# Column 128 moved beside the sine columns, with the padding of the weights gone and three steps moved

## The chip, the cores and the metric

The kernel runs on one core of a Trainium2 chip. The metric is the time of one execution in microseconds as the device measures it. The engines are named as in the profile: PE is the matrix engine (PEld its weight loads), DVE the vector engine, ACT the scalar engine, POOL the GpSimd engine, SP the queue that starts most transfers.

## The reference

For each of eight batches x is 3136 by 256 in float32. The reference takes the real part of the Fourier transform along both axes, and puts the result through a mixer: a low-rank step along the 3136 rows (rank 32, matrices U and V) and a two-layer perceptron along the 256 columns (hidden width 1024, ReLU), each with its residual.

```python
X = np.fft.fft(x, axis=1)
X = np.fft.fft(X, axis=2)
x = X.real.astype(np.float32)
...
xt = x.transpose(0, 2, 1)
h = xt @ U @ V
u = x + h.transpose(0, 2, 1)
ch = np.maximum(u @ w_ch1, 0.0) @ w_ch2
return (u + ch).astype(np.float32)
```

## The kernel before

The real part of a two-dimensional transform of real data is even under reflection, so sums and differences of mirrored elements ("folds") cut the work down. Along the 256 columns the folds leave 127 differences (sine columns) and 129 sums (cosine columns 0 to 128). Along the 3136 rows further folds split the data into quarters: `EOF_` and `EOR_` hold the column folds of the forward and reversed rows, `EOS` the next fold, `GE` and `GO` its even and odd halves, and `GC` (two tiles) the last fold of `GE`. PE then multiplies `GC` and `GO`, as weights of 128 columns, with tables of sines and cosines (`TABE`, `TABO`, `TABS`), on whose ends the transformed U is appended, so that the same products give the low-rank step's first factor.

The columns of the folded tiles are laid out as 0 to 127 sine (column 0 zero), 128 to 256 cosine 0 to 128, column 257 zero, and up to width `GW` = 384 zeros. The weights are taken in three groups: columns 0 to 127 (`typ` 0), 128 to 255 (`typ` 1), and 256 to 383, of which only column 256 holds data. The third group is used in `seq(b, 1, 0, .)`, `even_rows(b, 0, .)` and `u_alone(0, 0, .)`, directly behind products of `typ` 0, into the same PSUM tile.

The work is staged as follows. A front, written out in order (`tc.manual_schedule()`), makes the tables from `krow` by phases on DVE and sines on ACT, transforms U (`flip_u`, `fold_u`, `transform_u`), folds batch 0 and transforms it. On PE, `fill(n)` issues n matmuls whose result nobody reads, between the steps of the front. Behind it the output is made in 25 chunks of up to 512 folded rows. For each chunk c, `direct` and `mirrors` make the hidden layer (with `front` making the chunk's input u and `odd_part` the difference `uo` that `mirrors` reads), `second_product` the second layer, and `store` writes the result. Between these steps `turn(c, slot)` issues the steps that `put` filed under slot 6c + slot: the folds of later batches at the places in `FOLDS`, and the transform of a batch at the slots that `transform(b)` returns. Matmuls and the folds keep their program order; other operations are ordered by the framework's scheduler.

```python
iota(krow[:, 2 * NT:4 * NT], [[-2, 2 * NT]], 783)
...
todo = products(b, par, typ, P * typ, pn == 1, ne)
if typ == 0 and b == 0:
    todo = todo + products(b, par, 1, 256, (pn == 1) == (par == 1), ne)
elif typ == 0 and pn == 1:
    todo = todo + [(QW, w, rhs) for w, rhs in u_odd(b, 1, 256)]
```

All matmuls behind the front go through the helper at line 463, so in the profile they have one line and are told apart by tiles: pt and ptu are the transform's, pst the step along the columns, ph the low-rank step, p the two layers.

Of the kernel before, what the change touches and what calls it, by code (L numbers as in the profile page):

```python
# [27 lines left out]
GW = 384  # L28
# [3 lines left out]
def kernel(  # L32
# [94 lines left out]
    iota(krow[:, 2 * NT:4 * NT], [[-2, 2 * NT]], 783)  # L127
# [15 lines left out]
    iota(jv[:], [[1, KP]], 0, 1)  # L143
# [19 lines left out]
    for t in (EOF_, EOR_):  # L163
        nc.vector.memset(t.rearrange("p a i d -> p (a i) d")[:, :, 0:258:257], 0.0)
# [3 lines left out]

    def zeros(eng, s):
        eng.memset(GO[s].rearrange("p a i d -> p (a i) d")[:, :, 258:GW].bitcast(I32), 0)  # L170
        for c in range(2):
            eng.memset(GC[s][c][:, :, 258:GW].bitcast(I32), 0)

# [36 lines left out]
    def phase_even(i):  # L210

        y, col = phe[:, i // 2], ncol[:KP, i:i + 1]
        for part, src in ((slice(0, NT), strip(krow[:KP], NT // 2, [[NT, 2], [1, NT // 2]])),
                          (slice(NT, 2 * NT), krow[:KP, 3 * NT:4 * NT])):
            dst = y[:, part].bitcast(FP32)
            if part.start == 0:
                dst = dst.rearrange("p (a j) -> p a j", a=2)
            nc.vector.tensor_scalar(dst, src, col, float(2 ** (23 - 15)), op0=AL.mult, op1=AL.add)
        nc.vector.tensor_single_scalar(y, y, 2 ** 15 - 1, op=AL.bitwise_and)
# [24 lines left out]
    def flip_u():  # L244
        nc.vector.tensor_single_scalar(J[:], jv[:], 97.0, op=AL.is_equal)
        nc.vector.scalar_tensor_tensor(J[:], jv[:], 196.0, J[:], op0=AL.is_equal, op1=AL.add)
        pf = psum.tile([KP, 4, NI, R], FP32, tag="p1", name="pf", bufs=BUFS["p1"])
        nc.tensor.matmul(pf.rearrange("p q i r -> p (q i r)"), J[:],  # L248
                         UA.rearrange("p q i r -> p (q i r)"), start=True, stop=True)
        return pf  # L250

    def fold_u(UF):
        for t in range(2):
            op = AL.add if t else AL.subtract
            nc.vector.tensor_tensor(uy[:, t, 0].rearrange("p a (i r) -> p a i r", r=R),
                                    UF[:, 0:4:2], UR[:, 3::-2, ::-1], op=op)
            nc.vector.tensor_tensor(uy[:, t, 1].rearrange("p a (i r) -> p a i r", r=R),
                                    UR[:, 0:4:2, ::-1], UF[:, 3::-2], op=op)
# [58 lines left out]
    def transform_u(t, fill=None):  # L317
# [46 lines left out]
        def evict():  # L364
# [4 lines left out]
                                 pu[:KP, 6:8, :].rearrange("p c r -> p (c r)"), AF.Copy, scale=hv[:KP])  # L369
            nc.scalar.copy(TABO[t].rearrange("p n i w -> p (n i) w")[:PQ, :, 2 * NT:WO], pu[:PQ, 8:12, :])  # L370
# [3 lines left out]
        return even_k, odd_k, evict  # L374
# [41 lines left out]
    def along_d(qs, src, dst, part):  # L416
# [18 lines left out]
    def half(b, par, cols):  # L435
# [3 lines left out]
        if par and b:  # L439
            ins = nc.vector.tensor_copy(dst[:, :, :, 0], dst[:, ::-1, :, 256])  # L440
# [70 lines left out]
    def products(b, par, t, col, odd, ne):  # L511

        mm = []
        if par == 0:
            for c in range(2):
                g = GC[b % 2][0 if (c == 0) == (t == 1) else 1]
                lo, hi, at = ((0, TE - NT + ne, 0), (T2 - ne, WE, TE - NT))[c]
                for i in ((0, 2) if odd else (1, 3)):
                    mm.append((at, g[:kp(i), i, col:col + P], TABE[t][:kp(i), i, lo:hi]))
        else:  # L520
            for i in ((0, 2) if odd else (1, 3)):
# [4 lines left out]
                for nm in range(2):  # L526
                    mm.append((at, GO[b % 2][:kp(i), nm, i, col:col + P],
# [3 lines left out]
    def u_odd(b, t, col):  # L531

        todo = []
        for i in range(NI):
            tab, lo = (TABS[t], off_u(t, i)) if i % 2 else (TABO[t], 2 * NT)
            todo += [(GO[b % 2][:kp(i), nm, i, col:col + P], tab[:kp(i), nm, i // 2, lo:lo + NE])
# [3 lines left out]
    def add_up(pt, todo):  # L540
        for n, (at, w, rhs) in enumerate(todo):
            mm(pt[:, at:at + rhs.shape[-1]], w, rhs, start=(n == 0), stop=(n == len(todo) - 1),
               skip_group_check=True)

    def seq(b, par, typ, pn, tag="dft", part=True):
# [5 lines left out]
        todo = products(b, par, typ, P * typ, pn == 1, ne)  # L551
# [53 lines left out]
    def even_rows(b, typ, pn, tag="dft"):  # L605
# [6 lines left out]
        todo = products(b, 0, typ, P * typ, pn == 1, ne)  # L612
        if typ == 0:
            todo = todo + products(b, 0, 1, 256, pn == 0, ne)
        for n, (at, w, rhs) in enumerate(todo):
            mm(pt[:, at:at + rhs.shape[-1]], w, rhs, start=(pn == 0 and n == 0),
# [27 lines left out]
    def u_alone(b, typ, kept, odd=True, even=True):  # L644
# [4 lines left out]
        for t, col in ((1, P),) if typ else ((0, 0), (1, 256)):  # L649
            if odd:  # L650
                todo += u_odd(b, t, col)
            for c in range(2) if even else ():
                g = GC[b % 2][0 if (c == 0) == (t == 1) else 1]
                lo = TE - NT + NE * c
                todo += [(g[:kp(i), i, col:col + P], TABE[t][:kp(i), i, lo:lo + NE]) for i in range(NI)]
        at = typ * R
        for n, (w, rhs) in enumerate(todo):
            mm(kept["pt"][:, at:at + R], w, rhs, start=(odd and n == 0), stop=(even and n == len(todo) - 1),
# [5 lines left out]
    def even_first(b, typ):  # L664
# [3 lines left out]
        todo = products(b, 0, typ, P * typ, False, 0) + products(b, 0, typ, P * typ, True, 0)  # L668
# [5 lines left out]
    def even_again(b, typ, kept):  # L674
# [5 lines left out]
        add_up(pt, products(b, 0, typ, P * typ, False, 0))  # L680
# [276 lines left out]
    def transform(b):  # L957
# [19 lines left out]
        if b == 1:  # L977
            return 11, [a[:1], c0 + a[1:] + [lambda: apart(b, 1, pin=True)], c[1:] + d[:1], s[:1] + d[1:] + s[1:],
# [14 lines left out]
    def spread(t, i):  # L993

        return ([(both(t, i, 0, 0, 1, NT), 0, 2 * NT), (TABO[t][:, 0, i // 2, 0:2 * NT], 2 * NT, 4 * NT)]
# [4 lines left out]
    def piece(y, lo, hi, two):  # L1000
        return y[:, lo:hi].rearrange("p (c j) -> p c j", c=2) if two else y[:, lo:hi]
# [274 lines left out]
```

## Time and profile before

| | |
|---|---|
| median of 3 runs | 435.47 us (434.97 to 435.5) |
| the profiled execution | 435.61 us |
| its span, first to last instruction | 433.8 us |
| granted clock of PE | 1.000 |
| HBM traffic over the span | 126 GB/s |

A page of the profile gives the busy time of each engine, its groups of instructions and the chain of work that ended last. Timelines list instructions by start time, with duration, line and tile, and in brackets the idle time before them and what ended it. An entry with a count merges instructions that follow each other; its duration runs from the start of the first to the end of the last, and since matmuls overlap, the time to the next entry's start tells more than the duration. A form such as 98*128 98x229 is a weight of 98 rows and 128 columns with 229 streamed columns.

### The profile page before, as it was taken

To read this page: it belongs to the slowest core of one execution; us is meant where nothing else is said; L and a number is where in the kernel's file an instruction comes from. 1 tells how busy PE (TensorE), PEld (TensorE's weight loads), DVE (VectorE), ACT (ScalarE), POOL (GpSimd) and SP (SyncE) were. 2 spreads that over 40 slices of the span, in tenths; PEclk is the share of its full clock that TensorE was granted. 3 is DMA by queue.
4 is the path that set the end of the run, shared out by engine and by line. 5 is a ranking of instruction groups with operands and counts; after the bars stand their busy time and mean duration, and the time that the engine had idled before them with its cause. 6 is when DMAs were issued, how large, how long until landed. Compare 5 with 4: busy or idle time off the path is not lost.

```text
span 433.8 us, 9407 instructions
## 1 busy us (share of the span) xinstructions
PE 423.4 (98%) x3508; PEld 284.5 (66%) x3508; DVE 319.9 (74%) x667; ACT 292.4 (67%) x633; POOL 124.3 (29%) x340
## 2 busy tenths in 40 slices
PE   5999999999999999999999999999999999999996
PEld 2774666666766676676766666666766766666675
DVE  8998989896998887769787887679777554353442
ACT  7968765676667657676667657676667657765751
POOL 8943423132225223224233042232123010011111
PEclk9999999999999999999999999999999999999999
DMA  7899799868799387627885386976334324334543
GB/s 205 216 205 201 166 278 115 199 146 214 155 192 276 99 211 197 181 73 203 168 229 146 86 195 91 177 199 147 74 94 131 100 74 116 85 122 121 122 126 121
DMA packets 89166, 67.83 MB, mean 156 GB/s; under 512 B 55403, under 2 KB 82431, under 8 KB 89119
## 3 DMA queue, kind: packets, MB, share of 16 engines
q1 hardware_dynamic: 83350, 52.79, 51.4%
q0 software_dynamic: 5472, 14.36, 13.2%
q8 instruction: 27, 0.44, 0.4%
q14 instruction: 21, 0.16, 0.1%
q10 hardware_dynamic: 296, 0.07, 0.1%
HBM read 28.86 MB, written 25.69 MB: 126 GB/s over the span
## 4 chain that ended last, share of the span: by engine, by line
PE 93%; DVE 3%; ACT 2%; issue 0%; DVEq 0%; ACTq 0%
PE p L463 72%; PE pt L463 8%; PE pst L463 5%; PE fill L1049 3%; PE ph L463 2%; PE ptt L463 1%; ACT h L872 1%; PE pu L322 1%; PE pq L463 1%; PE ptu L463 0%; ACT h L888 0%; PE pf L248 0%; DVE u L458 0%; DVE pho L206 0%; PE psu L463 0%
## 5 line engine op out<-in xcount | busy, mean ns | idle before, releaser
L463 PE MATMUL p<-w,h 128*128 128x256 bf16 x1576 | 195.3, 273 | 0.0
L463 PEld LDWEIGHTS <-h 128*128 128x128 bf16 x1576 | 148.6, 98 | 39.6 <-issue 15.5
L888 ACT ACTIVATE h<-p 128x512 bf16<-128x512 f32 (+1 forms) x200 | 101.5, 595 | 82.3 <-PE p L463 80.2
L872 ACT ACTIVATE h<-p 128x512 bf16<-128x512 f32 (+1 forms) x200 | 101.7, 599 | 8.5 <-PE p L463 8.0
L463 PE MATMUL p<-u,w 128*128 128x512 bf16 (+1 forms) x400 | 92.8, 375 | 0.1
L950 DVE TENSOR_TENSOR o<-p,ut 128x256 f32<-128x256 f32 (+1 forms) x95 | 39.6, 417 | 70.4 <-PE p L463 47.2
L955 POOL TENSOR_TENSOR o<-o,fx 128x2 f32<-128x2 f32 (+1 forms) x95 | 40.2, 424 | 145.3 <-DVE o L951 79.6
L463 PEld LDWEIGHTS <-w 128*128 128x128 bf16 x512 | 41.8, 97 | 36.8 <-issue 0.3
L463 PE MATMUL p<-uo,wd 128*128 128x512 bf16 (+1 forms) x200 | 50.8, 375 | 0.6 <-DVE uo L458 0.4
L458 DVE TENSOR_TENSOR u<-ph,T 128x512 bf16<-128x512 f32 (+23 forms) x63 | 34.3, 556 | 9.2 <-PE ph L463 7.8
L951 DVE TENSOR_TENSOR o<-p,ut 128x256 f32<-128x256 f32 (+1 forms) x95 | 38.9, 410 | 0.0
L453 DVE TENSOR_TENSOR eor<-xr 99x1016 bf16<-99x1016 f32 (+1 forms) x34 | 38.5, 1145 | 0.6 <-DMA xr<-in_x_dram 0.6
L57 POOL DMA_INDIRECT xf<-in_x_dram,xidx x32 | 35.4, 1105 | 12.1 <-issue 7.4
L453 DVE TENSOR_TENSOR eof<-xf 99x1016 bf16<-99x1016 f32 (+1 forms) x33 | 38.4, 1172 | 0.0
L458 DVE TENSOR_TENSOR u<-ph,S 128x512 bf16<-128x512 f32 (+23 forms) x63 | 34.3, 555 | 0.9 <-PE ph L463 0.3
L846 POOL TENSOR_TENSOR fx<-ut 128x4 f32<-128x4 bf16 x48 | 14.6, 304 | 63.0 <-DMA ut<-u 63.0
L463 PEld LDWEIGHTS <-wd 128*128 128x128 bf16 x200 | 19.4, 98 | 13.6 <-issue 0.9
L463 PE MATMUL pt<-te,gc 98*128 98x229 bf16 (+1 forms) x196 | 24.4, 260 | 0.2
L463 PEld LDWEIGHTS <-gc 98*128 98x128 bf16 x220 | 19.2, 97 | 4.6 <-issue 0.9
L694 ACT CAST T<-pst 128x392 bf16<-128x392 f32 (+1 forms) x28 | 17.2, 615 | 7.4 <-PE pst L463 6.0
L845 POOL TENSOR_TENSOR fx<-ut 128x4 f32<-128x4 bf16 x24 | 7.3, 304 | 48.9 <-DMA ut<-u 48.9
L463 PEld LDWEIGHTS <-go 98*128 98x128 bf16 x216 | 16.5, 97 | 6.7 <-issue 0.4
(187 smaller groups left out, 459.5 us busy)
## 6 DMA issues: line engine op xcount, KB each, us to landing
out_dram<-o SPq DMA_DIRECT2D x33, 512.0 KB
xr<-in_x_dram SPq DMA_DIRECT2D x15, 784.0 KB
out_dram<-o SPq DMA_DIRECT2D x8, 384.0 KB
out_dram<-o SPq DMA_DIRECT2D x8, 256.0 KB
out_dram<-o SPq DMA_DIRECT2D x10, 128.0 KB
xr<-in_x_dram SPq DMA_DIRECT2D x2, 392.0 KB
ut<-u SPq DMA_TRANSPOSE x48
vv<-vv SPq DMA_DIRECT2D x3, 196.0 KB
```

What stands on the lines that cost most here:

```text
L57: nc.gpsimd.indirect_dma_start(out_, None, bass.AP(t.tensor, t.offset, [[w, rows], [1, w]]), bass.IndirectOffsetOnAxis(idx, 0), element_of ...
L453: ins = nc.vector.tensor_tensor(*a, **k)
L458: ins = nc.vector.tensor_tensor(*a, **k)
L463: ins = nc.tensor.matmul(*a, **k)
L694: eng(to, pt[:, :n])
L846: nc.gpsimd.tensor_tensor(fx[:, :, 1], ut[:, 0:n, 0] if hf else ut[:, n:2 * n, 0], ut[:, n + 1:2 * n + 1, 0], op=AL.subtract)
L872: nc.scalar.activation(k["h", 0][q][:, j - 4 * q, :w], p1[:, :w], AF.Relu)
L888: nc.scalar.activation(k["h", 1][q][:, g, :w], k["p1"][g][:, :w][:, ::-1], AF.Relu)
L950: nc.vector.tensor_tensor(o[:, ts, 0:P], p2[:, :w, 0:P], ut[:rows, ts, 0:P], op=AL.add)
L951: nc.vector.tensor_tensor(o[:, ts, P:D], p2[:, :w, P:D], strip(ut[:rows], (CH // P + t0 + 1) * P, [[P, w], [-1, P]]), op=AL.add)
L955: nc.gpsimd.tensor_tensor(o[:, ts, cols], o[:, ts, cols], fx[:rows, ts, 1 - hf:], op=AL.add)
L1049: nc.tensor.matmul(pt[:, 0:2 * NT], TABO[0][:PQ, 0, 1, 0:P], TABO[0][:PQ, 0, 0, 0:2 * NT], start=True, stop=True)
```

## The change

- Columns: the folded tiles now hold sine in 0 to 127, cosine column 128 in column 128, a zero in 129, and cosine 0 to 127 in 130 to 257. `GW` is 258, and the padding with its six memsets on POOL is gone. The third group of weights is two columns wide (128 and 129) instead of 128, and its products write two partitions.
- In the front, folds that took the sine columns and the last two in two operations take columns 0 to 129 in one (`half`, `fourth`). `phase_even` needs one operation instead of two for its phases, since `krow` is stored in another order (the odd tables' sines read it through an access pattern). `flip_u` builds its matrix with one comparison instead of two, from a `jv` made by two iotas, and multiplies in two halves; `fold_u` takes its sums in another order. `evict` is split in two functions called in the old order. `fill(15)` becomes `fill(10)`.
- Moved: the `uo` of chunk 4 is issued in chunk 3, behind `front(4, 0)`; batch 1's `fourth` goes from slot 10 to 10.75 and the first step of its transform from slot 11 to 12; the first fold of batch 2 from slot 13 to 13.75.

```diff
-GW = 384
+GW = 258
+COL = (0, 130, 128)
...
-    iota(krow[:, 2 * NT:4 * NT], [[-2, 2 * NT]], 783)
+    iota(krow[:, 2 * NT:4 * NT], [[-NT, 2], [-2 * NT, 2], [-2, NT // 2]], 783)
...
-    iota(jv[:], [[1, KP]], 0, 1)
+    iota(jv[:, 0:PQ], [[1, PQ]], 0, 1)
+    iota(jv[:, PQ:KP], [[0, 1]], -1, 1)
...
-        nc.vector.scalar_tensor_tensor(J[:], jv[:], 196.0, J[:], op0=AL.is_equal, op1=AL.add)
...
-            fold_tt(dst[:, qs, :, 129:256], lo, hi, op=AL.add)
+            fold_tt(dst[:, qs, :, 131:258], lo, hi, op=AL.add)
...
-        (eng or nc.gpsimd.tensor_copy)(dst[:, qs, :, 128:257:128], src[:, qs, :, 0:129:128])
+        (eng or nc.gpsimd.tensor_copy)(dst[:, qs, :, 130:127:-2], src[:, qs, :, 0:129:128])
...
+    def some(grp):
+
+        return slice(COL[grp], COL[grp] + (2 if grp == 2 else P))
...
-                    mm.append((at, g[:kp(i), i, col:col + P], TABE[t][:kp(i), i, lo:hi]))
+                    mm.append((at, g[:kp(i), i, cols], TABE[t][:kp(i), i, lo:hi]))
...
-            mm(pt[:, at:at + rhs.shape[-1]], w, rhs, start=(n == 0), stop=(n == len(todo) - 1),
+            mm(pt[:w.shape[-1], at:at + rhs.shape[-1]], w, rhs, start=(n == 0), stop=(n == len(todo) - 1),
...
-            todo = todo + products(b, par, 1, 256, (pn == 1) == (par == 1), ne)
+            todo = todo + products(b, par, 1, 2, (pn == 1) == (par == 1), ne)
...
-            todo = todo + [(QW, w, rhs) for w, rhs in u_odd(b, 1, 256)]
+            todo = todo + [(QW, w, rhs) for w, rhs in u_odd(b, 1, 2)]
...
-            return 11, [a[:1], c0 + a[1:] + [lambda: apart(b, 1, pin=True)], c[1:] + d[:1], s[:1] + d[1:] + s[1:],
+            return 11, [[], a[:1] + c0 + a[1:] + [lambda: apart(b, 1, pin=True)], c[1:] + d[:1], s[:1] + d[1:] + s[1:],
...
-    zeros(nc.gpsimd, 0)
-    zeros(nc.gpsimd, 1)
...
-    us[2]()
-    uc[2]()
+    for step in (us[2], us[3], uc[2], uc[3]):
+        step()
     nc.scalar.copy(W1[:, 1, :], w1t[:])
-    fill(15)
-    for cols in (slice(0, 128), slice(256, 258)):
-        half(0, 1, cols)
+    fill(10)
+    half(0, 1, slice(0, 130))
...
-    FOLDS = {1: (5, 5, 6, 6, 6, 7, 8, 12, 9, 9, 10, 10, 10.75),
-             2: (13, 13.75, 15, 15, 15, 16, 16, 16.75, 17, 19.75, 20, 20, 20, 21, 21, 22.75, 22.75),
+    FOLDS = {1: (5, 5, 6, 6, 6, 7, 8, 12, 9, 9, 10, 10.75, 10.75),
+             2: (13.75, 13.75, 15, 15, 15, 16, 16, 16.75, 17, 19.75, 20, 20, 20, 21, 21, 22.75, 22.75),
...
-        if c > 1:
+        if c > 1 and c != 4:
             odd_part(c)
...
         if c + 1 < NCH:
             front(c + 1, 0)
+        if c == 3:
+            odd_part(c + 1)
```

More of the change, by code (lines that the diff above doesn't have):

```diff
@@ L167 @@
           for s in range(2)]
[L169 to L172, printed above, removed]
     def const(v):
@@ L212, in phase_even @@
         y, col = phe[:, i // 2], ncol[:KP, i:i + 1]
[L213 to L218, printed above, removed]
+        nc.vector.tensor_scalar(y.bitcast(FP32).rearrange("p (a j) -> p a j", a=4),
+                                strip(krow[:KP], NT // 2, [[NT, 4], [1, NT // 2]]), col, float(2 ** (23 - 15)),
+                                op0=AL.mult, op1=AL.add)
         nc.vector.tensor_single_scalar(y, y, 2 ** 15 - 1, op=AL.bitwise_and)
@@ L509, in four, with products @@
         return strip(t, at, [[0, P // R], [1, R]])
-    def products(b, par, t, col, odd, ne):
-        mm = []
+    def some(grp):
+        return slice(COL[grp], COL[grp] + (2 if grp == 2 else P))
+    def products(b, par, t, grp, odd, ne):
+        mm, cols = [], some(grp)
         if par == 0:
@@ L654, in u_alone @@
                 lo = TE - NT + NE * c
-                todo += [(g[:kp(i), i, col:col + P], TABE[t][:kp(i), i, lo:lo + NE]) for i in range(NI)]
+                todo += [(g[:kp(i), i, some(col)], TABE[t][:kp(i), i, lo:lo + NE]) for i in range(NI)]
         at = typ * R
         for n, (w, rhs) in enumerate(todo):
-            mm(kept["pt"][:, at:at + R], w, rhs, start=(odd and n == 0), stop=(even and n == len(todo) - 1),
+            mm(kept["pt"][:w.shape[-1], at:at + R], w, rhs, start=(odd and n == 0), stop=(even and n == len(todo) - 1),
                skip_group_check=True)
@@ L1088 @@
     mirror(1, slice(0, 128), AL.subtract)
-    mirror(1, slice(256, 258), AL.add)
+    mirror(1, slice(128, 130), AL.add)
     fill = filler()
@@ L1106 @@
     sin_odd = dict(ST[0])
-    for cols in (slice(0, 128), slice(256, 258)):
-        half(0, 0, cols)
-        for c in range(2):
-            fourth(0, c, cols)
+    half(0, 0, slice(0, 130))
+    for c in range(2):
+        fourth(0, c, slice(0, 130))
     U0 = {}
@@ L1123 @@
     nc.gpsimd.memset(msr[:, :, 1:2], 1.0)
-    mirror(1, slice(128, 256), AL.add)
-    half(0, 1, slice(128, 256))
+    mirror(1, slice(130, 258), AL.add)
+    half(0, 1, slice(130, 258))
     seq(0, 1, 1, 0, "dft", False)
```

63 lines of the change are left out of this document (34 added, 29 removed).

## The prediction

> **What bounds the kernel now.** I read the page's head and its busy shares first, then the windows of the stages, then the waits of TensorE (PE), and last the timelines of the front.
>
> ```profile
> span 433.8 us, 9407 instructions
> ...
> PE 423.4 (98%) x3508; PEld 284.5 (66%) x3508; DVE 319.9 (74%) x667; ACT 292.4 (67%) x633; POOL 124.3 (29%) x340
> ```
>
> ```profile
> 0.00:22.40 22.40, 17.18 (x137) 10.68 (x138) 21.03 (x52) 19.80 (x55) 19.52 (x41) 1.00 0.79 207
> ...
> 130.00:420.00 290.00, 290.00 (x2377) 195.31 (x2374) 199.54 (x423) 194.85 (x407) 71.69 (x211) 1.00 0.57 142
> ```
>
> The columns of a window are its length, the busy time of PE, weight loads, DVE, ACT and POOL with their counts, then granted clock, DMA share and GB/s. From 130 to 420 us PE is busy for all of 290.00 us at clock 1.00. What lengthens or shortens the PE stream there goes into the end time one for one; work of DVE, ACT and POOL does not, as long as PE doesn't wait for it. In the first 22.4 us it is the other way round: DVE is busy 21.03 of 22.40 us, and PE fills its time with dummy matmuls. PE's waits behind the start are four short ones; these two touch the change (the sum, the count and the longest):
>
> ```profile
> PE p L463 <- DVE uo L458: 0.4, 1, 0.4
> ...
> PE pt L463 <- DVE A L639: 0.2, 1, 0.2
> ...
> ```
>
> So there are two places where the change can gain (the front, and some of these waits) and one where it can lose: the PE stream itself.
>
> **The front: fewer dummy matmuls and fewer DVE operations.** The timelines of PE and DVE there:
>
> ```profile
> 15.24 3.14 PE L1049 MATMUL fill<-to 98*128 98x392 bf16 x18
> 18.22 0.23 PE L322 MATMUL pu<-guo,ts 99*98 99x32 bf16 x2
> ...
> 19.75 2.81 PE L1049 MATMUL fill<-to 98*128 98x392 bf16 x16
> 22.40 0.84 PE L463 MATMUL pt<-ts,go 98*128 98x196 bf16 x8
> ```
>
> ```profile
> 4.90 0.26 DVE L246 SCALAR_TENSOR_TENSOR jx<-jv,jx 99x99 f32<-99x99 f32 x1
> ...
> 10.85 2.33 DVE L453 TENSOR_TENSOR eor<-xr 99x1016 bf16<-99x1016 f32 x2
> 13.22 2.35 DVE L453 TENSOR_TENSOR eof<-xf 99x1016 bf16<-99x1016 f32 x2
> ...
> 21.14 0.78 DVE L453 TENSOR_TENSOR go<-eos 99x1024 bf16<-99x1024 bf16 x2
> 21.83 0.68 DVE L453 TENSOR_TENSOR ge<-eos 99x1024 bf16<-99x1024 bf16 x1
> ```
>
> A fill costs (22.40-19.75)/16 = 0.166 us. Five fewer bring PE to its first real product at 22.40-0.83 = 21.57, and the flip of U, released by one DVE operation less (0.26), at about 21.3. But that product reads go, which DVE ends at 21.14+0.78 = 21.92. How much earlier does DVE come there? Ahead of 10.85 it loses the 0.26 us operation, and two pairs of 196-element operations become single ones of 392, which saves less than that again: some 0.35 in all. That does not reach go, for the fold at 13.22 reads xf, and xf lands then:
>
> ```profile
> 3.88 0.97 POOL L57 DMA_INDIRECT xf<-in_x_dram,xidx  x1 [0.30 <-issue]
> ```
>
> ```profile
> xf<-in_x_dram,xidx POOLq DMA_INDIRECT x1, 9.3
> ```
>
> The second gather (all issues between 3.7 and 5 us) starts at 3.88 and lands 9.3 us later, at 13.18: DVE is just in time now, and would wait if it came earlier. POOL has one small iota more ahead of the gathers and one with three strides, so the landing may come 0.1 later instead. Behind 13.22 DVE saves the small half of the go pair (0.78 for two against 0.68 for the same form alone, 0.1 less a few ns). So go ends between 21.8 and 21.95, the first product starts at about 22.0, and the gain is **-0.40 us**. Its bounds: 0 if the gathers slip further, -1.1 if DVE's whole saving arrived. The two small ge and gc operations removed behind it give DVE another 0.3 us that PE, then in its 16 products, doesn't wait for.
>
> The POOL memsets of the padding go too; they were off PE's path, and what stands behind them in POOL's queue (the lone columns, the loads of V and the weights, batch 1's gathers) moves up. The reordered phases and sines keep their element counts; the evictions of U, split in two, run in their old order; batch folds keep their sizes, with columns renamed. All these lie beside PE: nothing for them, and DVE, ACT and POOL have 26% or more of idle time in the span to cover a few ns each.
>
> **Columns 128: the narrow weights.** Here the PE stream changes. The old weights for column 128 were 128 columns wide, mostly zeros; the new ones are two wide (g[:, 128:130]), and their products write two partitions. The number of matmuls and of streamed columns stays. What could change is the matmul rate, and the step into and out of such a group. The trace holds one group of narrow weights, the last chunk's eight rows (128*8), and groups with 32 rows:
>
> ```profile
> 420.04 1.92 PE L463 MATMUL p<-w,h 128*128 128x256 bf16 x16
> 421.79 1.06 PE L463 MATMUL p<-u,w 128*128 128x264 bf16 x8
> ...
> 425.19 1.92 PE L463 MATMUL p<-w,h 128*128 128x256 bf16 x16
> ...
> 427.04 0.49 PE L463 MATMUL p<-w,h 128*8 128x256 bf16 x3
> 427.15 0.49 PE L463 MATMUL p<-w,h 128*8 128x256 bf16 x3
> ```
>
> ```profile
> 427.04 0.75 PEld L463 LDWEIGHTS <-h 128*8 128x8 bf16 x8 [0.21 <-issue]
> ```
>
> Sixteen wide products take 421.79-420.04 = 1.75 us, 0.109 each. From 425.19 the same sixteen should hand over at 426.94; the first narrow one starts at 427.04, 0.10 late. Inside the group the pace is 427.15-427.04 = 0.11, as for wide weights: two columns instead of 128 make no matmul faster. The load row says why the start is late: 0.21 us of idle in front of it with nothing to wait for ("issue"), that is, it was not loaded under the matmul before. The same stands at every group of 32 rows:
>
> ```profile
> 59.60 1.89 PE L463 MATMUL p<-u,w 128*128 128x512 bf16 x8
> 61.33 0.56 PE L463 MATMUL pt<-ts,go 98*128 98x228 bf16 x4
> ...
> 65.31 1.03 PE L463 MATMUL p<-uo,wd 128*128 128x512 bf16 x4
> 66.27 0.40 PE L463 MATMUL p<-dv,qf 32*128 32x512 bf16 x4
> 66.50 0.38 PE L463 MATMUL ph<-vv,ta 32*128 32x512 bf16 x2
> 66.81 1.92 PE L463 MATMUL p<-w,h 128*128 128x256 bf16 x16
> ```
>
> A 512-column product takes (61.33-59.60)/8 = 0.216. Four are 0.865, and the step into 32 rows comes after 0.96: 0.095 late. Out of it, the two ph run side by side in 0.216, and the next comes after 0.31: 0.094 late. Between the two 32-row groups (66.27 to 66.50) there is 0.23, no such step. Weights of 98 columns do not pay it: 18 fills ahead of the 98*98 group take (18.22-15.24)/18 = 0.166 each, like those ahead of a wide group. So the price is on changing between the whole array and a narrow part of it. Two columns are nearest to the eight-column row, and I take 0.0975 a step, 0.195 for a group entered and left. Bounds: 0.10 for a group if only the entry pays (the way out of the 128*8 group is hidden in the trace), 0.33 if each step waited until the record of the matmul before ends (0.273 less 0.109):
>
> ```profile
> L463 PE MATMUL p<-w,h 128*128 128x256 bf16 x1576 | 195.3, 273 | 0.0
> ```
>
> The Trainium skill, TensorEngine Tiling (Array Packing), section Tiling Modes, says that changing the tiling mode, not merely the tile, drains the engine. By a full drain the step would be that upper bound; the rows of this trace show 0.10, and I go by them.
>
> How many groups? In the code, each batch from 1 on has one in each of even_rows(b, 0, 0) and even_rows(b, 0, 1) (four products each) and one in seq(b, 1, 0, 1) (eight 32-column products of u_odd): 3 x 7 = 21. Each lies between whole-array products, so none shares a step. Batch 0 has five: both seq(0, 1, 0, .), both even_rows(0, 0, .), and u_alone(0, 0). That is 26 x 0.195 = **+5.07 us**, all on PE's path: the 21 in the saturated stretch, the five behind the first product at 22.0, from where PE feeds ACT and DVE without slack.
>
> The 32-column products may also lose pace:
>
> ```profile
> 12.05 0.52 PE L322 MATMUL pu<-guo,to 98*98 98x32 bf16 x8
> 12.41 0.34 PE L322 MATMUL pu<-guc,te 98*98 98x32 bf16 x4
> ...
> 25.30 0.35 PE L463 MATMUL ptu<-te,gc 98*128 98x32 bf16 x8
> 25.50 0.20 PE L463 MATMUL ptu<-to,go 98*128 98x32 bf16 x2
> ```
>
> Wide weights give 0.20/8 = 0.025, weights of 98 columns 0.36/8 = 0.045. For two columns I take 0.025 (the 8-column pace showed no loss); at 0.045 the 72 of them (8 a batch for seven batches, 16 in u_alone) add 1.4 us. The Trainium skill, TensorEngine Tiling (Array Packing), section Tile-to-Partition Mapping, lists the fast weight load among what column tiling disables. That speaks for the slower pace; no trace here shows it for two columns.
>
> **The moved steps.** Chunk 4's uo: PE waits 0.41 us for it.
>
> ```profile
> 100.84 1.02 PE L463 MATMUL p<-uo,wd 128*128 128x512 bf16 x4 [0.41 <-DVE uo L458]
> ```
>
> ```profile
> 57.25 1.30 DVE L453 TENSOR_TENSOR gc<-ge 99x1032 bf16<-99x1032 bf16 x2
> 58.47 0.68 DVE L458 TENSOR_TENSOR u<-ph,S 128x512 bf16<-128x512 f32 x1
> ```
>
> ```profile
> 57.19 1.92 PE L463 MATMUL p<-w,h 128*128 128x256 bf16 x16
> 59.20 0.56 PE L463 MATMUL pt<-te,gc 98*128 98x229 bf16 x4
> ```
>
> Issued in chunk 3, uo stands in DVE's queue ahead of batch 2's go instead of behind an output addition: **-0.41**. It puts one operation of some 0.4 us in front of gc and go of batch 2; PE waits for neither now (the list has no such wait), so I put nothing; without that spare it would cost those 0.4. Batch 1's gc, moved behind u, lets u free its PSUM tiles some 1.2 us sooner; the first even product of batch 1 took such a tile at 59.20, just after u's first half, 0.26 behind the sixteen products from 57.19 (57.19+1.75 = 58.94). That product itself moves one slot, behind direct, since gc is later now; ACT then copies it behind the four ReLUs instead of in front, so its chain to A ends about as before, and the 0.2 us wait for A stays. I put **-0.2**. Batch 2's first fold goes behind an output addition; PE doesn't wait for it: 0.
>
> **Sum.** The profiled execution took 435.61 us (span 433.8 and 1.81 around it); the median of the runs is 435.47, 0.14 less. 435.61 - 0.40 + 5.07 - 0.41 - 0.2 = 439.67, less 0.14: **439.5 us**.
>
> **Rivals.** (a) *The narrow weights cost no step.* If two columns are loaded under the matmul before like 98 are, the 5.07 goes and 435.47 - 1.01 = 434.5 is left: faster. For it: 98*98 pays nothing. Against it: 128*8 and 32*128 do. It decides below 1.01/26 = 0.04 us a group. Chance 0.08. (b) *Only the entry pays*, or half of the steps hide: 26 x 0.10 gives 437.1. Chance 0.12. (c) *Every step drains fully*: 26 x 0.33 = 8.6 in place of 5.07, 443.0. Against it stand the three steps measured above. Chance 0.05. The Trainium skill's rule on the tiling mode, taken word for word, is this case. (d) *The front loses*: POOL, freed of six memsets in a stage in which it is busy 19.52 of 22.40 us, issues V and the weights while the last of batch 0's x is arriving (DMA share 0.79 over the front), and DVE, busy 94% there, waits up to 1 us: 440.5. Chance 0.12. The forecast, with the slower 32-column pace inside it as its upper end (440.9), has 0.63.
>
> **Numbers.** The range is 437.1 to 441.5: from (b) to (d) with some of the slower pace; outside lie (a), (c) and the outer parts of (b) and (d). A measurement of this kernel can tell 0.2%, about 0.9 us. Faster by that is most of (a), 0.07; within it the rest of (a) and partial sums near it, 0.05; slower 0.88.
>
> **What would show it.** In the profile after: weight loads of form 98*2 with an "issue" idle in front of each group's first; the te,gc group of eight in a batch no longer evenly paced but about 0.2 us longer; a batch's period on PE 0.6 us longer (three groups); the first pt product at about 22.0 with PE idle before it, released by go; no PE wait on uo at chunk 4. A stretch from 130 to the end as long as before would prove the main term wrong; a period longer by over 1 us would prove it too small.

## The result, and the profile after

| | before | after |
|---|---|---|
| median (runs) | 435.45 us (434.97 to 435.5, 6) | 440.75 us (440.36 to 446.17, 6) |
| profiled execution | 435.61 us, span 433.8 | 440.36 us, span 438.6 |
| ratio | | 1.0149, interval 1.0111 to 1.0186 |

The changed kernel is slower. Its median lies 5.3 us above that of the kernel before, where the forecast had 4.1. The ratio is higher than the medians' own (1.0122): two of the six executions took 444.87 and 446.17 us at mean clocks of 0.988 and 0.983, and that is why it points to 441.9 us, just above the range. Where those two come from is followed up below.

The page's head, then the windows after (their columns are those of the prediction's windows):

```profile
span 438.6 us, 9387 instructions
...
PE 427.2 (97%) x3505; PEld 280.3 (64%) x3505; DVE 319.1 (73%) x660; ACT 293.1 (67%) x633; POOL 125.9 (29%) x335
```

```profile
0.00:22.40 22.40, 16.72 (x134) 10.72 (x134) 19.75 (x47) 19.33 (x54) 18.93 (x35) 1.00 0.80 205
...
130.00:420.00 290.00, 290.00 (x2348) 190.27 (x2347) 199.65 (x425) 194.17 (x404) 73.66 (x209) 1.00 0.59 139
```

PE is still busy for all 290 us of the long stretch at clock 1.00, but it gets through 2348 recorded matmuls there instead of 2377. DVE is busy 1.28 us less in the front (19.75 against 21.03), and PE's first product still comes later. The chain that ended last shows the first half of this best, by a piece of 24 matmuls that recurs once a batch (start, length, what):

```profile
128.60 3.58 PE p L463 x24
177.53 3.58 PE p L463 x24
```

```profile
130.09 3.58 PE p L458 x24
179.59 3.58 PE p L458 x24
```

The first fence is before, 48.93 us a batch; the second is after, 49.50. A batch has grown by 0.57 us, 0.19 for each of its three narrow groups (forecast 0.195). The timeline of PE shows one of them, and below it the same place before:

```profile
69.92 1.05 PE L458 MATMUL pt<-te,gc 98*128 98x229 bf16 x8
70.90 1.02 PE L458 MATMUL pt<-to,go 98*128 98x424 bf16 x6
71.77 0.20 PE L458 MATMUL pt<-ts,go 98*2 98x32 bf16 x2
71.82 0.20 PE L458 MATMUL pt<-to,go 98*2 98x32 bf16 x2
...
72.00 1.06 PE L458 MATMUL pt<-te,gc 98*128 98x229 bf16 x8
```

```profile
68.83 0.96 PE L463 MATMUL pt<-te,gc 98*128 98x229 bf16 x8
69.63 0.92 PE L463 MATMUL pt<-to,go 98*128 98x424 bf16 x6
70.39 0.20 PE L463 MATMUL pt<-ts,go 98*128 98x32 bf16 x2
...
70.55 0.95 PE L463 MATMUL pt<-te,gc 98*128 98x229 bf16 x8
```

Eight te,gc products, four of them narrow, take 70.90-69.92 = 0.98; before, the eight with wide weights took 0.80. The 32-column products on two columns keep their pace (0.05 for two, 71.77 to 71.82): the loss is at the edges of the group. Entering the three pairs took 71.77-70.90 = 0.87 (0.76 before), and from there to the next wide group 0.23 (0.16 before). The loads by form say the same:

```profile
L458 PEld LDWEIGHTS <-gc 98*128 98x128 bf16 x110 | 9.8, 97 | 4.1 <-issue 1.4
...
L458 PEld LDWEIGHTS <-gc 98*2 98x2 bf16 x54 | 3.6, 82 | 3.3 <-issue 3.0
```

A narrow load is shorter (82 ns against 97), but 54 of them have 3.0 us of "issue" idle ahead, twice what 110 wide ones have.

The front, on PE, DVE and POOL, and PE's waits:

```profile
19.67 1.98 PE L1049 MATMUL fill<-to 98*128 98x392 bf16 x11
22.72 0.94 PE L458 MATMUL pt<-ts,go 98*128 98x196 bf16 x8 [1.07 <-DVE go L448]
```

```profile
10.50 2.34 DVE L448 TENSOR_TENSOR eor<-xr 99x1016 bf16<-99x1016 f32 x2
13.96 2.36 DVE L448 TENSOR_TENSOR eof<-xf 99x1016 bf16<-99x1016 f32 x2 [1.13 <-issue]
...
21.97 0.70 DVE L448 TENSOR_TENSOR go<-eos 99x1040 bf16<-99x1040 bf16 x1
```

```profile
4.23 1.03 POOL L58 DMA_INDIRECT xf<-in_x_dram,xidx  x1 [0.30 <-issue]
```

```profile
PE pf L241 <- DVE jx L238: 4.6, 1, 4.6
PE pt L458 <- DVE go L448: 1.1, 1, 1.1
PE pt L458 <- ACT ev L619: 0.5, 1, 0.5
PE pu L314 <- ACT ts L409: 0.4, 1, 0.4
PE psu L458 <- ACT A L671: 0.3, 1, 0.3
PE pst L458 <- ACT S L726: 0.2, 1, 0.2
```

DVE is at its folds 0.35 us sooner, as worked out (10.85 to 10.50). Then it stands idle for 1.13 us. The row says "issue" here, but the fold reads xf, and by the trace xf has just landed, at 13.88, as it had ahead of the fold before (13.14 and 13.22). go ends at 22.67. PE's first product is 0.32 us later than before, behind 1.07 us of idle time. The wait on uo is gone; a new one, on ACT's ev, has come.

Where the 4.8 us of the two spans lie (after less before, between the same products on PE):

| stretch | forecast | measured |
|---|---|---|
| up to the first product (22.40, 22.72) | -0.40 | +0.32 |
| to the uo products at 55.69 and 56.96: batch 0's five groups | +0.98 | +0.95 |
| to 65.31 and 66.65: batch 1's moved slots | -0.2 | +0.07 |
| to 127.04 and 128.53: six groups and the uo wait | +0.76 | +0.15 |
| to the last uo products (424.44, 428.81): fifteen groups | +2.93 | +2.88 |
| to the end of the span (433.81, 438.56) | 0 | +0.38 |

Two rows are small because of the execution shown of before. In the third it took 9.62 us; seven other profiles of kernels with the old slots take 9.35 to 9.37 there, the six with the moved slots 9.69 to 9.71, so the move costs 0.33 in that stretch. The fourth row is small because the execution shown of before lost 0.8 us in that stretch: it took 61.73 us there, the second experiment below, with the same wide weights, 60.92, and the changed kernel 61.88.

### The profile page after: what moved, and what is told of

Same layout as the page of the kernel before. It is cut to its first block, busy times and chain, and to the rows that moved or that the text cites. A ratio compares the mean times of both kernels' runs of the same rounds, so it can differ in the third digit from the quotient of the medians.

```text
span 438.6 us, 9387 instructions
## 1 busy us (share of the span) xinstructions
PE 427.2 (97%) x3505; PEld 280.3 (64%) x3505; DVE 319.1 (73%) x660; ACT 293.1 (67%) x633; POOL 125.9 (29%) x335
## 4 chain that ended last, share of the span: by engine, by line
PE 91%; ACT 2%; DMA 2%; DVE 2%; POOL 1%; issue 1%; POOLq 0%; ACTq 0%
PE p L458 73%; PE pt L458 9%; PE pst L458 4%; PE ph L458 2%; DMA xf<-in_x_dram,xidx 2%; ACT h L871 1%; PE ptt L458 1%; DVE eof L448 1%; PE pq L458 1%; DVE eor L448 1%; ACT h L887 0%; DVE eos L448 0%; PE ptu L458 0%; POOL xf L58 0%; PE psu L458 0%
## 5 line engine op out<-in xcount | busy, mean ns | idle before, releaser
L58 POOL DMA_INDIRECT xf<-in_x_dram,xidx x32 | 36.5, 1141 | 11.7 <-issue 6.9
L845 POOL TENSOR_TENSOR fx<-ut 128x4 f32<-128x4 bf16 x48 | 14.7, 307 | 60.8 <-DMA ut<-u 60.7
L458 PE MATMUL pt<-te,gc 98*128 98x229 bf16 (+3 forms) x196 | 25.9, 260 | 0.5 <-ACT ev L619 0.5
L458 PEld LDWEIGHTS <-gc 98*128 98x128 bf16 (+1 forms) x220 | 17.1, 92 | 8.5 <-issue 4.3
L458 PEld LDWEIGHTS <-go 98*128 98x128 bf16 (+1 forms) x216 | 15.1, 92 | 9.9 <-issue 3.5
```

The lines of the kernel that those rows point to most:

```text
L58: nc.gpsimd.indirect_dma_start(out_, None, bass.AP(t.tensor, t.offset, [[w, rows], [1, w]]), bass.IndirectOffsetOnAxis(idx, 0), element_of ...
L458: ins = nc.tensor.matmul(*a, **k)
L845: nc.gpsimd.tensor_tensor(fx[:, :, 1], ut[:, 0:n, 0] if hf else ut[:, n:2 * n, 0], ut[:, n + 1:2 * n + 1, 0], op=AL.subtract)
```

## The experiments

**Narrow weights alone.** The kernel before, its layout and zeros kept, with only the third group's weights and output cut to two.

```
+    def wid(col):
+        return 2 if col == 256 else P
-    mm.append((at, g[:kp(i), i, col:col + P], ...))
+    mm.append((at, g[:kp(i), i, col:col + wid(col)], ...))
```

> The kernel before with one edit: the third group of weights (column 256) is two columns wide instead of 128, and its products write two partitions; layout, padding, front and slots stay. Theory 1 (each narrow group pays a step into and one out of the narrow part of the array, 0.19 us a group): 21 groups of batches 1 to 7 and five of batch 0 give +4.9 us, 440.3 us; the period of a batch on PE goes from 48.92 to 49.50. Rival 1 (the loss comes from the new layout, rows of 516 bytes and weights that start at odd places): no change, 435.4, period 48.92. On the spread of the executions after the change (four at 440.4 to 440.9 at a mean clock of 0.998 or more, two at 444.9 and 446.2 at 0.988 and 0.983): if PE's idle of 1.07 us ahead of its first product lowers the clock later, all executions of this kernel keep clock 1.00, since PE has no such gap here; if the narrow groups do, some of them fall to 0.98 to 0.99 and take 5 us longer.

Measured: 440.4 us (439.79 to 440.8, 5 runs) beside 435.36 us before, ratio 1.0103 (1.0081 to 1.0125). The chain:

```profile
130.04 3.58 PE p L463 x24
179.54 3.58 PE p L463 x24
```

49.50 us a batch, exactly the changed kernel's. Two columns in place of 128 give +5.0 us with nothing else changed; layout and moved steps have no part in it.

**The change without narrow weights.** The changed kernel, its third group 128 columns wide again. In that layout there are no zeros beside column 128, so the third group's products add other columns to the rows behind the first two; only the time is read.

```
-        return slice(COL[grp], COL[grp] + (2 if grp == 2 else P))
+        return slice(2, 2 + P) if grp == 2 else slice(COL[grp], COL[grp] + P)
```

> The kernel after with one edit: the third group of weights is again 128 columns wide (columns 2 to 129, all of them initialised), so that every product of the transform uses the whole array; the 126 surplus rows add foreign terms to the sums, so the output isn't the reference's, and only the time counts. Theory 1: the 26 groups lose their steps, period 48.92 instead of 49.50, and 440.75 less 4.9 is 435.9; what is then left against before is the front and the moved steps, about +0.4 or less. Rival 1 (layout): 440.7, period 49.5. On the spread: if PE's idle ahead of its first product is the cause, some executions still show a clock of 0.98 to 0.99; if the narrow groups are, none does.

Measured: 436.05 us (435.58 to 440.37, 12 runs), ratio 1.0038 (1.0013 to 1.0063). Eight executions lie at 435.6 to 436.8, four at 439.1 to 440.4. The chain shows the old period, 48.93:

```profile
128.22 3.58 PE p L458 x24
177.15 3.58 PE p L458 x24
```

So the rest of the change, forecast at -1.0, brings nothing: in the eight lower executions about 0.5 us are lost against 435.36.

**Weights 64 wide.** As the first, with 64 columns.

```
-        return 2 if col == 256 else P
+        return 64 if col == 256 else P
```

> The kernel before with the third weight group 64 columns wide in place of 128 (2 of them used, 62 zeros; the output lands on 64 partitions). Theory P, that every load narrower than the array's full width makes the step in and out: period of a batch 49.4 to 49.6 us, 440.2 to 440.6 us as with 2 columns. Theory Q, that the step belongs to tiles of at most 32 columns: period 48.93 us and 435.2 to 435.6 us. A period between them (about 49.2) would mean that the step's price goes with the width.

Measured: 441.3 us (440.91 to 442.24, 4 runs), ratio 1.0138 (1.0122 to 1.0155).

```profile
130.25 3.58 PE p L463 x24
179.88 3.58 PE p L463 x24
```

49.63 us a batch: 0.70 more than with 128, 0.23 a group. The load row of this form has the same idle time ahead and a longer load than two columns or 128:

```profile
L463 PEld LDWEIGHTS <-gc 98*64 98x64 bf16 x54 | 4.7, 109 | 3.0 <-issue 2.8 <-DVE eof L453 0.2
```

It is not the number of columns saved that counts. Of the three widths, 64 columns cost more than two, and 128 columns of mostly zeros are the cheapest. Why 64 cost more than two is not shown.

**Chunk 4's uo alone**, moved as in the change, in the kernel before.

```
-        if c > 1:
+        if c > 1 and c != 4:
             odd_part(c)
...
+        if c == 3:
+            odd_part(c + 1)
```

> The kernel before with one thing moved: uo of chunk 4 is made at the end of chunk 3. If the idle time of 0.57 us that PE had ahead of chunk 4's uo products was a real gap of the stream, the time falls by 0.4 to 0.6 us, to 434.8 to 435.0 us, PE's waits show none on uo and all else stands. The rival: the wait only stands for PE's own lag, or the earlier operation delays another of DVE's that PE needs, and the time stays at 435.2 to 435.6 us.

Measured: 435.16 us (434.96 to 436.09, 12 runs) beside 435.42, ratio 0.9995 (0.9983 to 1.0007): no difference that can be told. DVE's timeline of the kernel before, in the profiled execution, shows why (the output addition ahead of uo):

```profile
99.62 0.42 DVE L950 TENSOR_TENSOR o<-p,ut 128x256 f32<-128x256 f32 x1 [2.08 <-PE pt L463]
...
100.37 0.42 DVE L458 TENSOR_TENSOR uo<-S,T 128x512 bf16<-128x512 bf16 x1
```

In two other kernels with uo in its old place the same two operations stand so (ten dummy matmuls first, then the slots alone):

```profile
97.48 0.42 DVE L950 TENSOR_TENSOR o<-p,ut 128x256 f32<-128x256 f32 x1 [0.17 <-PE pt L463]
...
98.22 0.42 DVE L458 TENSOR_TENSOR uo<-S,T 128x512 bf16<-128x512 bf16 x1
```

```profile
98.51 0.42 DVE L950 TENSOR_TENSOR o<-p,ut 128x256 f32<-128x256 f32 x1 [0.50 <-DMA out_dram<-o]
...
99.26 0.41 DVE L458 TENSOR_TENSOR uo<-S,T 128x512 bf16<-128x512 bf16 x1
```

The addition waited 2.08, 0.17 and 0.50 us, in the last by the profile for a store of the output. uo came 1 to 2 us sooner in these two, and neither has a wait of PE on uo. The kernels with narrow weights alone, with 64 columns and with no dummy matmul ahead of the first product, whose uo is in its old place too, have none either. The 0.41 us belonged to the one profiled execution more than to the code.

**The slots alone** (batch 1's first even step and gc fold, batch 2's first fold) in the kernel before.

```
-            return 11, [a[:1], c0 + a[1:] + [...], ...
+            return 11, [[], a[:1] + c0 + a[1:] + [...], ...
-    FOLDS = {1: (..., 9, 9, 10, 10, 10.75), 2: (13, 13.75, ...
+    FOLDS = {1: (..., 9, 9, 10, 10.75, 10.75), 2: (13.75, 13.75, ...
```

> The kernel before with only the slots moved: batch 1's first even step and its gc fold one slot later, batch 2's first fold three quarters of a slot later. Prediction on record: -0.2 us. The other reading, from the new wait of 0.47 us on ACT's ev copy that the changed kernel shows in slot 12: that wait is the move's own, appears here at about 62.5 us too, and the time is 0.1 to 0.4 us above the kernel with nothing moved (435.5 to 435.8 us). The period of a batch stays 48.93 us in both.

Measured: 435.83 us (434.8 to 436.56, 11 runs) beside 435.31, ratio 1.0001 (0.9989 to 1.0013). By the times this is no difference. By the trace the move has a price:

```profile
62.70 0.56 PE L463 MATMUL pt<-te,gc 98*128 98x229 bf16 x4 [0.47 <-ACT ev L620]
```

That is the changed kernel's new wait, in a kernel where nothing but the slots differs. From the uo products at 56.30 to those at 126.89, a stretch that holds the move and no wait on uo, PE takes 70.59 us. The kernel with only uo moved takes 70.34 there (56.22 to 126.56), that with ten dummy matmuls 70.45 (55.72 to 126.17). So 0.1 to 0.25 us are lost, not 0.2 gained.

The gain had no ground either. The prediction took it from the first even product of batch 1, which started 0.26 us late at 59.20 (2.01 us behind the start of the sixteen products from 57.19). With the same slots, the kernel with only uo moved has these two starts at 57.71 and 59.47 and that with ten dummy matmuls at 57.21 and 58.97: 1.76 us, no delay.

**The iotas.** The changed kernel with the old index rows, phase operations and flip matrix, so that the gathers are issued as early as before.

```
-    iota(krow[:, 2 * NT:4 * NT], [[-NT, 2], [-2 * NT, 2], [-2, NT // 2]], 783)
+    iota(krow[:, 2 * NT:4 * NT], [[-2, 2 * NT]], 783)
-    iota(jv[:, 0:PQ], [[1, PQ]], 0, 1)
-    iota(jv[:, PQ:KP], [[0, 1]], -1, 1)
+    iota(jv[:], [[1, KP]], 0, 1)
```

> The kernel after with the tables' index code of before: krow in the old order with its one-stride iota, jv in one iota with two comparisons, phase_even with two operations each; all else stays. Theory: in the profile after, POOL starts the first two gathers at 2.61 and 4.23 us instead of 2.44 and 3.88, their data lands about 0.7 us later, and DVE waits 1.13 us for it (fold at 13.96 instead of 13.22). With the old code the fold is back at 13.2 to 13.3, go ends some 0.7 us earlier, the first product starts at about 22.0 instead of 22.72, and the time falls by 0.6 to 0.7 us against the kernel after, to about 440.0. Rival (DVE's operations, not the landing, set the fold): the two operations put back make it later by 0.35 us, 441.1.

Measured: 440.56 us (439.36 to 446.24, 6 runs), ratio 1.01 (1.0077 to 1.0123) without the execution at 446.24. The median is the changed kernel's (440.75) within the noise; neither the 440.0 of the theory nor the 441.1 of the rival came.

```profile
3.89 0.98 POOL L58 DMA_INDIRECT xf<-in_x_dram,xidx  x1 [0.31 <-issue]
```

```profile
13.81 2.35 DVE L451 TENSOR_TENSOR eof<-xf 99x1016 bf16<-99x1016 f32 x2 [0.59 <-DMA xf<-in_x_dram,xidx]
...
19.68 1.29 DVE L451 TENSOR_TENSOR eor<-xr 99x508 bf16<-99x508 f32 x2 [0.52 <-DMA xr<-in_x_dram]
```

The second gather is issued at 3.89 as before (4.23 in the changed kernel), and the fold still waits until 13.81. A second wait, on xr, follows at 19.68, and PE's first product comes at 23.17, later than in the changed kernel. The iotas are not the whole of it. Over all profiles the fold on xf starts at 13.1 to 13.8 us in nine kernels with the old iotas (in two of these DVE came too late to wait, in three it waited 0.1 us or less; the last kernel below, which puts other folds ahead, is left out) and at 13.9 to 14.7 in four with the new ones. So the later issue goes with a later landing, but the landing also moves by over half a microsecond from one execution to the next.

**The dummy matmuls.** Two kernels put 17 and 15 of them into the changed kernel, two put 10 and none into the kernel before.

```
-    fill(10)
+    fill(17)        # then: fill(15)
```

> The kernel after with fill(17) in place of fill(10), so that PE's idle ahead of its first product (21.65 to 22.72 in the profile after) is filled by seven more dummy matmuls of 0.166 us. Theory on the spread, idle: no execution falls below clock 0.995, and the time is 440.4 to 440.9 plus at most 0.2 us, since the product waits for go anyway. Rival, narrow groups: the spread stays, some executions at 444 to 446. If neither, the spread depends on nothing in these kernels and may show in any of the four.

> The changed kernel with the 15 dummy matmuls that the kernel before has there, in place of 10. Theory A: no execution at a lower clock, all at 440.3 to 441.2 us (the first product no more than 0.1 us later than with 10), so the ratio falls to 1.011 to 1.013 with a narrow interval. Rival B: one execution in four is still at a mean clock below 0.997 and at 444 us or more.

```
-    fill(15)
+    fill(10)        # then: fill(0)
```

> The kernel before with 10 in place of 15 dummy matmuls ahead of the first product. PE then stands idle for some 0.4 to 0.8 us until go. Theory A, that this idle time is what brings the changed kernel its executions at a lower mean clock: about a quarter to a third of the executions are 3.5 to 6 us slow with a mean clock of 0.983 to 0.996, the rest at 434.9 to 435.5 us. Rival B, that these come from another part of the change (layout, fewer DVE operations): every execution at 434.7 to 435.5 us and clock 0.998 to 1.0.

> The kernel before with no dummy matmul ahead of the first product in place of 15, so that PE is idle for 2.2 us or more there. Theory A: half or more of the executions show a mean clock below 0.997 and are 3.5 to 6 us slow (439 to 441 us), and if the profiled execution is among them its windows show where the clock is lower. Rival B: 434.7 to 435.5 us in every execution at clock 0.998 to 1.0.

| kernel | median (range, runs) | ratio (interval) |
|---|---|---|
| after, 17 | 441.41 (441.03 to 441.73, 4) | 1.0127 (1.0102 to 1.0153) |
| after, 15 | 440.74 (440.62 to 441.09, 6) | 1.0114 (1.0096 to 1.0132) |
| before, 10 | 435.28 (434.53 to 439.97, 12) | 1.0011 (0.9984 to 1.0039) |
| before, none | 438.41 (437.51 to 440.58, 6) | 1.0072 (1.0049 to 1.0096) |

With 15 the changed kernel keeps its median and loses its high executions. With 10 the kernel before gets them: four of twelve at 437.7 to 440.0. With none it has nothing else, at mean clocks of 0.992 to 0.996 in all six. Counting as high what lies 3 us or more above its kernel's fastest: of all kernels with 10 dummy matmuls, 11 of 36 executions; of those with 13 or more, none of 123, the highest 2.9 us above. (The last kernel below, with another cause for its idle time, is left out.) The narrow weights have no part in this: alone, with 15 dummy matmuls, they have none in five, while the wide weights of the second experiment, with 10, have four in twelve. The profiled execution with none shows what happens (timeline of PE, then windows, granted clock in the third column from the right):

```profile
21.93 1.38 PE L463 MATMUL pt<-ts,go 98*128 98x196 bf16 x8 [1.19 <-DVE go L453]
...
25.60 0.85 PE L463 MATMUL pt<-te,gc 98*128 98x197 bf16 x8
```

```profile
20.60:21.93 1.33, 0.14 (x1) 0.03 (x1) 1.33 (x5) 1.33 (x9) 1.33 (x1) 1.00 0.97 172
21.93:23.00 1.07, 1.07 (x8) 1.00 (x9) 1.03 (x3) 1.00 (x1) 0.77 (x2) 0.56 0.83 84
```

PE is idle for 1.19 us, and behind that the granted clock is half from 22.06 to 25.47, for 3.41 us. The first sixteen products take 25.60-21.93 = 3.67 us instead of 2.01 (22.40 to 24.41 before). In the changed kernel no execution at the low clock was profiled; its two high ones have the low mean clocks, so there the same cause is likely, not shown. In the kernel before with 10, three of the four high ones have mean clocks of 0.998 to 1.0: for these the clock is not the explanation, or not all of it, and it stays open.

Two things did not come as expected. The changed kernel with 15 still waits 0.9 us for go, since xf landed later still in that execution (fold at 14.65), and it has no high execution; the profiled execution with the old iotas kept the full clock over 1.24 us of idle time, longer than the 1.19. So the idle time's length alone doesn't decide. And 17 cost 0.7 us against the changed kernel's median, though its first product came at 22.86: its profile has a new wait of PE, for DVE's A ahead of the products into psu (0.6 us).

The clock in these traces shows what else counts. It changes only at the ends of steps of 3.41 us: the stretches at full clock ahead of the half one and behind it are 10.24 and 409.6 us, 3 and 120 steps. Here are the step ahead of the fall and, from the last kernel below, the step in which PE's idle time of 2.75 us begins:

```profile
18.64:22.06 3.42, 2.23 (x33) 1.77 (x32) 3.38 (x8) 3.39 (x15) 3.15 (x4) 1.00 0.91 223
22.06:25.47 3.41, 3.41 (x16) 2.10 (x15) 3.31 (x8) 1.36 (x2) 1.44 (x3) 0.50 1.11 147
```

```profile
20.29:23.70 3.41, 1.86 (x12) 0.88 (x9) 3.38 (x7) 2.67 (x11) 3.14 (x4) 1.00 0.94 224
23.70:27.12 3.42, 2.22 (x19) 1.70 (x20) 3.35 (x11) 0.49 (x1) 1.36 (x3) 1.00 1.12 208
```

PE counts as busy for longer in the first, but most of its products there stream only 32 columns. Counted at the pace of the dummy matmuls (392 columns in 0.166 us), the streamed columns fill 0.40 of the step from 18.64 and 0.50 of that from 20.29. In the 14 profiles the clock fell behind every full-clock step filled to 0.40 or less (all but this one lie at the end of the span, where PE runs out of work) and behind none filled to 0.43 or more. The 1.07 us of the changed kernel stand in a step filled to 0.60, the 1.24 us with the old iotas in one filled to 0.53, and the 2.75 us are spread over two, of 0.50 and 0.64. The first whole step at full clock begins between 9.4 and 11.8 us in these profiles, so the same idle time can lie in one step in one execution and across two in the next. That this is what makes some executions of a kernel long is not shown.

**Two versions meant to beat both.** First, the kernel before with uo moved and 13 dummy matmuls; then that with the single phase operations (and the order of `krow` that they need), and DVE's folds of xr quarter 0 ahead of those that wait for xf.

```
-    fill(15)
+    fill(13)
...
+    for part in range(2):
+        along_d(one(0), xr, EOR_, part)
     for part in range(2):
         along_d(EV, xf, EOF_, part)
```

> A version meant to beat both: the kernel before with uo of chunk 4 moved and 13 dummy matmuls in place of 15 ahead of the first product. Expected 434.7 to 435.1 us: the uo move as measured (435.16) and up to 0.33 us for the two dummy matmuls where go is there by 22.1 us. If idle time of under 0.4 us ahead of the first product already brings slow executions, some of these lie at 437.6 us or more.

> The last one with the changed kernel's single phase operations (two DVE operations less) and with DVE's two folds of xr quarter 0 put ahead of the folds that wait for the gather xf, so that DVE has work until the gather lands. If the gather's landing (13.1 to 14.7 us in the runs so far) is what holds go, DVE stands idle under 0.2 us ahead of the xf folds, go ends at 21.5 to 21.8 us even for a landing at 14 us, and the time is 434.6 to 435.0 us. If xr quarter 0 lands later than the gather, the wait moves to it and go ends at 22 us or later: 435.2 us or more.

The first: 435.25 us (434.45 to 436.08, 12 runs) beside 435.31, ratio 0.9999 (0.9989 to 1.0009). No high execution, no gain that can be told. The second: 438.83 us (437.3 to 439.53, 5 runs), ratio 1.008 (1.0066 to 1.0095). DVE's timeline says why:

```profile
11.57 2.34 DVE L450 TENSOR_TENSOR eor<-xr 99x1016 bf16<-99x1016 f32 x2 [0.66 <-DMA xr<-in_x_dram]
16.16 1.28 DVE L450 TENSOR_TENSOR eor<-xr 99x508 bf16<-99x508 f32 x2 [2.25 <-DMA xr<-in_x_dram]
```

Quarter 0 of xr lands at 16.1 us, xf at 13.4 by the trace. DVE waits 2.25 us for xr, and PE waits 2.75 us for go. The old order of the folds follows the order of these landings. Nothing tried here beats the kernel before.

## Why the prediction was right and where it failed

**Direction and main term: right.** 26 groups at 0.195 us were put at 5.07. The trace has 0.95 for batch 0's five and 2.88 for the fifteen of batches 3 to 7, 0.19 each; narrow weights alone took +5.04 us. Rivals (a) and (b) fall: the step is paid on the way in (0.11 in the group shown) and on the way out (0.07). Rival (c), the full drain at 0.33, falls as well. The Trainium skill, TensorEngine Tiling (Array Packing), section Tiling Modes, says that a change of the tiling mode drains the engine. A group entered and left costs 0.19 us here at two columns and 0.23 at 64, less than a full drain by the matmul's record would. The runs fit the event that the rule names, and give its price; that it is a change of mode which these weights bring about, no run shows.

**32-column products: right** at 0.025 us; the 1.4 us of the upper bound didn't come.

**The front: wrong in sign, -0.40 against +0.32.** The step that failed is "the landing may come 0.1 later". DVE's saving ahead of the fold came as worked out, and went into a wait: the fold on xf could start at 13.96, 9.7 us after an issue that was itself 0.35 later (before, 9.3 us after it). One landing of one execution had been taken for a constant. Rival (d) had DVE waiting up to 1 us, and it did wait 1.13; but POOL's earlier loads are not shown as the reason. The gathers themselves went out later, and the landing wanders by execution.

**Chunk 4's uo: right on the wait, wrong on the gain.** The wait is gone, but it was a property of one execution (an output addition that stood 2.08 us on that occasion); moved alone it brings 0.26 us, which is within the noise.

**Batch 1's slots: wrong, -0.2 against +0.1 to +0.25.** The prediction saw that ACT copies the first even product "behind the four ReLUs instead of in front" and looked only at A. PE's next te,gc product waits for that same copy, 0.47 us. The wait for A, which was to stay, is gone in return (0.16 us). And the term's price was a draw like the one on uo: the late start at 59.20 stands in the one profiled execution alone.

**Not foreseen: the tail and the clock.** From the last uo products to the end of the span the changed kernel takes 0.38 us longer, without a narrow weight in that stretch that wasn't there before. Its last rows on DVE and POOL show the small addition starting later behind DVE:

```profile
433.83 0.28 DVE L950 TENSOR_TENSOR o<-p,ut 128x128 f32<-128x128 f32 x1
434.54 0.20 POOL L954 TENSOR_TENSOR o<-o,fx 128x2 f32<-128x2 f32 x1 [1.31 <-DVE o L950]
```

By the trace 0.42 us lie between DVE's end and POOL's start; before, it was 0.13 (429.65 to 429.78). From the start of ACT's last copy to the end of the span the changed kernel takes 4.05 us, its variants with wide weights, 15 and 17 dummy matmuls 4.04 to 4.05, that with the old iotas 3.84; the kernel before takes 3.67 and its variants with narrow weights or a moved uo 3.67 and 3.66. The 0.42 stands in the same place in the three variants with 4.04 to 4.05, and in none of the others. Why is open.

The dummy matmuls carried the result past the upper end of the range, and this is the step of the front term that failed beside the landing: the prediction booked five fewer of them as time saved, foresaw "PE idle before" the first product, and put that idle time at nothing. In its place some executions become 3 to 6 us longer, and those lift the measured ratio: 1.0149 with 10, that is 441.9 us, against 1.0114 with 15, which would be 440.4 us, inside the range. Half clock for a step behind idle time is shown for one execution; for the two long ones here it is likely, and for others open. The rest (0.7 us on the front, 0.4 on the tail, no gain from the moved steps) took the median from the forecast 439.5 to 440.75, still inside.

## What to carry to other kernels

Narrowing a group of weights among wide ones saved no time on the streaming side here and cost a step on the way in and one on the way out, 0.19 us a group: in a saturated PE stream, padding to the width of the neighbouring groups was cheaper. A wait or a landing in one profile is one draw; before an edit is credited with removing it, see whether other executions have it at all. Dummy matmuls that look too many may be what covers a variable landing, and in part what holds the clock: taking five out moved the spread, not the median.

## What the runs showed of the hardware that was not expected

The granted clock fell to 0.50 behind 1.19 us of idle PE and stayed there for 3.41 us. In another execution, the profiled one of the last experiment, 2.75 us of idle time left it at 1.00 (four others of that kernel had mean clocks of 0.994 to 0.996). The Trainium skill, TensorE: Matmul & The Clock Gate, section HAM oscillation — how this bites in real kernels, gives idle gaps of over some 3.4 us as what brings the clock down. Here a third of that was enough once, and more than twice as long was not another time; the measurement decides. What separated the two is how much PE streamed in the step of 3.41 us that the gap lies in: 0.40 of it where the clock fell, 0.50 and 0.64 where it stayed. So a gap ahead of the first products is a risk well below the page's figure where the products before it are short.

A load of 64 columns takes 109 ns, longer than one of 128 (97) or of 2 (82), and its group costs the most, 0.23 us.
